# One engine instruction over two PSUM banks: four double tiles in place of eight single banks

## The chip, the cores and the metric

The kernel runs on one core of a Trainium2 chip. The metric is the device time of one execution in microseconds; lower is better. Engines are named as in the profile: PE (TensorE, matmuls), PEld (its weight loads), DVE (VectorE), ACT (ScalarE), POOL (GpSimd), SP (SyncE).

## What is computed

Sigmoid attention, then a gated feed-forward network over all tokens:

```python
batch, n_heads, seq, head_dim = (8, 12, 448, 64)
scale = 1.0 / np.sqrt(q.shape[-1])
scores = scale * np.matmul(q, k.transpose(0, 1, 3, 2)) - np.log(S)
attn = 1.0 / (1.0 + np.exp(-scores))
attn_out = np.matmul(attn, v)
x = attn_out.transpose(0, 2, 1, 3).reshape(B * S, H * D)      # 3584 x 768
gate = np.maximum(x @ w_gate, 0.0)                            # w_gate, w_val: 768 x 1536
val = x @ w_val
out = gate * val @ w_out                                      # w_out: 1536 x 768
```

Inputs and output are fp32; the kernel works in fp16 with fp32 accumulation in PSUM.

## The kernel before

The order on every engine is the program's own (`manual_schedule`); the framework adds the semaphores. A tile that takes over a buffer waits for the last accesses to the tile that held it before.

**PSUM.** There are eight banks of 512 fp32 per partition. During batch 0 four of them form a ring of single banks, `ring0`, and the other four are two double tiles of the pool `pairp`, for sigmoids over two banks (`FirstSlot.unit`, L270). At L634 `pairp` is closed and four further single banks, `ring1`, are opened in its place. From then on `bank(name)` hands out eight single banks in turn, and `later(order)` puts banks that stay in use for long at the end of the queue.

**Attention, batches 1 to 7.** The 12 heads are three groups of four. A *unit* (`qk_unit`, L292) makes the scores of one group against one seventh of the keys: four matmuls of 64x64 weights and 448 columns, which run beside each other in the array, into two banks; then ACT takes the sigmoid of each bank (L187). After seven units, `pv` (L242) multiplies by v with 28 such matmuls into two banks, and DVE copies each to `xT` (L184), scaled. The very last copy of batch 7 runs on ACT.

**Feed-forward.** Batches 0 and 1 (and 2) use `gv` (L304): six matmuls into a bank for the gate, six into another for the value, ReLU on ACT (L318) into `gate_sb`, and the product on DVE (L327) into `hT`. Later groups of two batches use `gv_pair` (L498): seven products of 2x2 blocks in place of eight, for two column blocks at once, in three pairs of banks `u`, `g2`, `g1` (in the code `b`, `c`, `a`), of which `b` is written four times. ACT or DVE copy (L524), DVE adds (L528), and DVE multiplies the gate by the value (L533), two instructions each, one for each bank. The sums of weights and tokens that this scheme needs (L376, L409, L479) are DVE's too. The output product is `down` (L341, banks `ya` and `yb`) or the seven-product `down_pair` (L423, banks `u`, `y12`, `y11`).

**The mix.** From batch 3 on, four or five units (with a `pv` after the second in every second stretch) are followed by one piece of feed-forward work, so that ACT works off its sigmoids while PE does large products. A `gv_pair` is 42 matmuls of 448 columns, a `down_pair` 42 of 384. In batches 1 and 2 the pieces are `gv`s (`ffn_mix`), and the sums of `w_out` (`weight_sums`) are queued on DVE between them as the weights come in. `gate_sums` runs on DVE once, in batch 3. `hold` makes POOL wait for a transposing DMA before it issues the next loads.

The queue of banks after a `gv_pair` is: two free banks, then `a`, `c`, `b`. After a `down_pair` it is: five free banks, then `a`, `c`, `b`.

Of the kernel before, what the change touches and what calls it, by code (L numbers as in the profile page):

```python
# [10 lines left out]
FP32 = mybir.dt.float32  # L11
# [6 lines left out]
def kernel(  # L18
# [36 lines left out]
    xTp = ctx.enter_context(tc.tile_pool(name="xTp", bufs=3))  # L55
    hTp = ctx.enter_context(tc.tile_pool(name="hTp", bufs=1))
    ysbp = ctx.enter_context(tc.tile_pool(name="ysbp", bufs=4))
    gsbp = ctx.enter_context(tc.tile_pool(name="gsbp", bufs=6))
    first_sbuf = ExitStack()
    early = first_sbuf.enter_context(tc.tile_pool(name="early", bufs=1))  # L60
    first_psum = ExitStack()
    free = deque()

    def open_banks(name):
        pool = ctx.enter_context(tc.tile_pool(name=name, bufs=1, space=bass.MemoryType.PSUM))
        free.extendleft((pool, f"{name}_{i}") for i in range(3, -1, -1))

    open_banks("ring0")
    pairp = first_psum.enter_context(
        tc.tile_pool(name="pairp", bufs=2, space=bass.MemoryType.PSUM)  # L70
    )
# [9 lines left out]
    def bank16(name):  # L81
        return bank(name, (P, 1024), FP16)

    def later(order):
        keys = [free[i - 8] for i in order]
        for key in keys:
            free.remove(key)
            free.append(key)

    in_tiles = {}
# [81 lines left out]
        for _ in range(count):  # L174
            nc.tensor.matmul(ps[:, 0:S], zeros[:, 0:P], zeros[:], start=True, stop=True)

    def put_xT(b, pr, q0, qn, src):
        if b not in xT_tiles:
            xT_tiles[b] = xTp.tile([P, NPAIR, S], FP16, tag="xT", name="xT")
        xT = xT_tiles[b][:, pr, q0 : q0 + qn]  # L180
        if b == B - 1 and pr == NPAIR - 1:
            nc.scalar.activation(xT, src, AF.Copy, scale=XSCALE)
        else:
            nc.vector.tensor_scalar(out=xT, in0=src, scalar1=XSCALE, scalar2=None, op0=AOP.mult)  # L184

    def sigmoid(PT_ap, ps_ap):
        nc.scalar.activation(PT_ap, ps_ap, AF.Sigmoid, bias=sig_bias, scale=qk_scale)  # L187


    def qkT_of(b, g):  # L190
        if (b, g) not in qkT_tiles:
            qkT_tiles[(b, g)] = qkTp.tile([P, TW, P], FP16, tag="qkT", name="qkT")
        return qkT_tiles[(b, g)]

    def pe_transposes(b, g, ti, c0=0, c1=NCH):
        t16 = in_tiles[b][ti]
        qkT = qkT_of(b, g)
        trt = bank16("trt")
        for c in range(c0, c1):
            for h in range(2):  # L200
                nc.tensor.transpose(
                    trt[64 * h : 64 * h + 64, c * P : (c + 1) * P],
                    t16[:, 2 * g + h, c * D : (c + 1) * D],
                    ident[:],
                )
# [35 lines left out]

    def pv(b, g, q0, qn, pieces):  # L242
        v16 = in_tiles[b][2]
        ps = [bank("pv_ps") for _ in range(2)]
        for c in range(NCH):
            for hh in range(2):
                for r in range(2):
                    o = row_of(r, hh)
                    rows = slice(o, o + 64)
                    nc.tensor.matmul(  # L250
                        ps[hh][64 * r : 64 * r + 64, 0:qn],
                        v16[rows, 2 * g + hh, c * D : (c + 1) * D],
                        pieces[c][rows, hh, :],
                        start=(c == 0),
                        stop=(c == NCH - 1),
                        tile_position=(o, 64 * r),
                        skip_group_check=True,
                    )
        for hh in range(2):
            put_xT(b, 2 * g + hh, q0, qn, ps[hh][:, 0:qn])  # L260


    class FirstSlot:
# [26 lines left out]
    PT_tiles = {}  # L290

    def qk_unit(b, g, c):  # L292
        ps = [bank("qk_ps") for _ in range(2)]
        qk(qkT_tiles[(b, g)], c, 0, NCH, lambda hh: ps[hh][:, 0:S])
        PT = PTp.tile([P, 2, S], FP16, tag="PT", name="PT")
        for hh in range(2):
            sigmoid(PT[:, hh, 0:S], ps[hh][:, 0:S])
        PT_tiles[(b, g, c)] = PT

    def pv_group(b, g):  # L300
# [1 line left out]


    def gv(b, q0, qn, f, act_relu):  # L304
        ps = []
        for nm, wt in (("g_ps", wg), ("v_ps", wv)):
            ps.append(bank(nm))
            for dc in range(NDC):
                nc.tensor.matmul(  # L309
                    ps[-1][:, 0:qn],  # L310
                    wt[:, dc, f * P : (f + 1) * P],
                    xT_tiles[b][:, dc, q0 : q0 + qn],
                    start=(dc == 0),
                    stop=(dc == NDC - 1),
                )
        gate_sb = gsbp.tile([P, S], FP32, tag="gsb", name="gate_sb")
# [10 lines left out]
        nc.vector.tensor_tensor(  # L327
            out=hT_tiles[g][:, f, o : o + qn],
            in0=gate_sb[:, 0:qn],
            in1=ps[1][:, 0:qn],  # L330
            op=AOP.mult,
        )
# [7 lines left out]

    def down(g, t):  # L341
        ysb = ysbp.tile([P, DM], FP32, tag="ysb", name="ysb")
        for nm, m0, m1 in (("ya", 0, 512), ("yb", 512, DM)):
            ps = bank(nm)
            for f in range(NFC):
                nc.tensor.matmul(  # L346
                    ps[:, 0 : m1 - m0],
                    hT_tiles[g][:, f, t * P : (t + 1) * P],
                    wo[:, f, m0:m1],
                    start=(f == 0),  # L350
                    stop=(f == NFC - 1),
                )
# [70 lines left out]
    def down_pair(g, p, beside, then, last, first_copy):  # L423
# [3 lines left out]
        B11, B21, B22 = wo[:, 0:HF, 0:HM], wo[:, HF:NFC, 0:HM], wo[:, HF:NFC, HM:DM]  # L427
        y1, y2 = (ysbp.tile([P, DM], FP32, tag="ysb", name="ysb") for _ in range(2))
        lo, hi = slice(0, HM), slice(HM, DM)
        b, c, a = bank("u"), bank("y12"), bank("y11")  # L430
        later((7, 6, 5))

        def product(ps, A, W, first=True):
            products([(ps, HM, HF, A, W, first)])
# [63 lines left out]
    def gv_pair(g, f, beside, first_copy):  # L498
        x1, x2 = xT_tiles[2 * g], xT_tiles[2 * g + 1]
        T1, T2, T4 = (late["X"][:, i] for i in range(3))  # L500
        B11, B21, T3, B22 = x1[:, 0:HD], x1[:, HD:NDC], x2[:, 0:HD], x2[:, HD:NDC]
        b, c, a = ([bank(nm) for _ in range(2)] for nm in ("u", "g2", "g1"))
        later((6, 7, 4, 5, 2, 3))
        gs = [[gsbp.tile([P, S], FP32, tag="gsb", name="gsb") for _ in range(3)] for _ in range(2)]
        if g not in hT_tiles:
            hT_tiles[g] = hTp.tile([P, NFC, 2 * S], FP16, tag="hT", name="hT")
        h = hT_tiles[g]
        sets = []
        for u in range(2):
            us, fs = slice(u * P, (u + 1) * P), slice((f + u) * P, (f + u + 1) * P)  # L510
            S1, S2, S4 = (t[:, :, us] for t in sums[("w", g, f)])
            sets.append((
                wg[:, 0:HD, fs], wg[:, HD:NDC, fs], wv[:, HD:NDC, fs],
                S1, S2, wv[:, 0:HD, fs], S4,
            ))
        del sums[("w", g, f)]

        def product(ps, i, W, first=True):
            for u in range(2):
                products([(ps[u], S, HD, sets[u][i], W, first)])  # L520

        def copy(i, ps, by=nc.scalar.copy):
            for u in range(2):
                by(gs[u][i][:], ps[u][:, 0:S])  # L524

        def plus(i, ps):
            for u in range(2):
                nc.vector.tensor_tensor(  # L528
                    out=gs[u][i][:], in0=ps[u][:, 0:S], in1=gs[u][i][:], op=AOP.add
                )  # L530

        def gated(u, o, gate_sb, val):
            nc.vector.scalar_tensor_tensor(  # L533
                out=h[:, f + u, o : o + S], in0=gate_sb, scalar=0.0, in1=val, op0=AOP.max, op1=AOP.mult
            )

        product(b, 0, B11)
        copy(0, b, first_copy)
        product(c, 3, T1)
        copy(2, c)  # L540
        product(b, 4, T2, False)
        copy(1, b)
        beside()
        product(a, 1, B21)
        plus(0, a)
        product(b, 5, T3, False)
        plus(2, b)
        product(c, 6, B22, False)
        plus(1, c)
        product(b, 2, T4, False)  # L550
        for u in range(2):
            gated(u, 0, gs[u][0][:], b[u][:, 0:S])
        for u in range(2):
            gated(u, S, gs[u][1][:], gs[u][2][:])

    gv_queue = deque()

# [73 lines left out]
        if b < 2:  # L631
            push_gv(b, 0, S, range(NFC))

    first_psum.close()  # L634
    open_banks("ring1")

    def hold(b, g):
        nc.gpsimd.tensor_copy(gate[0:1, :], qkT_tiles[(b, g)][0:1, 0, 0:2])
# [156 lines left out]
```

## Time and profile before

| | |
|---|---|
| median of 3 runs | 401.06 us (400.89 to 401.36) |
| span of the profiled execution, first to last instruction | 399.2 us |
| PE busy | 388.9 us (97%) |
| DVE busy | 279.9 us (70%) |
| ACT busy | 223.0 us (56%) |
| mean granted TensorE clock | 0.999 |

The profile gives the profiled execution's span alone; its own time is not listed, and what lies around the span is taken from the median: 401.06 - 399.2 = 1.86 us.

In the profile a line of a group names the line of the kernel, the engine, the operation, the tiles written and read, their shape, the count, and after the bar the busy time in us, the mean ns of one, and the idle time before them with what ended it. A line of the timeline gives the start in us from the beginning of the span, the length in us of the merged stretch, and the instruction with its count. A line of waits gives who waited for whom: us in total, times, and the longest. A busy PE is not PE at its peak, since the ends of matmuls are modelled; starts are recorded.

### The profile page before, as it was taken

How to read it: one execution, taken by the hardware profiler on the slowest of the kernel's cores; microseconds unless marked ns; L12 is line 12 of the kernel's file. 1: busy time of each engine (PE TensorE's matmuls, PEld its weight loads, DVE VectorE, ACT ScalarE, POOL GpSimd, SP SyncE). 2: the span in 40 equal slices, each digit the busy share in tenths (PEclk: the TensorE clock that was granted, in tenths of full speed). 3: DMA queues.
4: the chain of work that ended last, by engine and by line, in shares of the span. 5: the costliest groups of instructions: out<-in, count | busy, mean ns of one | idle time of the engine just before them, and what ended most of it. 6: DMA issues, size and time to landing. Idle time of an engine off the chain costs nothing.

```text
span 399.2 us, 8737 instructions
## 1 busy us (share of the span) xinstructions
PE 388.9 (97%) x3488; PEld 217.9 (55%) x3488; DVE 279.9 (70%) x539; ACT 223.0 (56%) x475; POOL 49.4 (12%) x73
## 2 busy tenths in 40 slices
PE   8999999999998999999999999999999999999994
PEld 3678786545455554554555555455455555555562
DVE  2454344367358889999758889999766779887661
ACT  5946778783885565655665455565566234533131
POOL 8643301600030300003000300000000000000000
PEclk9999999999999999999999999999999999999999
DMA  9999994999897894224945695223012320000144
GB/s 149 199 199 204 205 141 94 177 203 187 178 161 152 165 204 76 46 48 51 178 85 133 130 218 89 48 24 61 12 40 80 80 79 2 0 2 0 39 115 124
DMA packets 68793, 43.69 MB, mean 109 GB/s; under 512 B 35856, under 2 KB 65296, under 8 KB 68752
## 3 DMA queue, kind: packets, MB, share of 16 engines
q0 software_dynamic: 30736, 23.33, 39.1%
q1 hardware_dynamic: 37584, 19.24, 23.0%
q8 instruction: 27, 0.44, 0.5%
q10 hardware_dynamic: 432, 0.56, 0.4%
q14 instruction: 14, 0.11, 0.1%
HBM read 47.19 MB, written 11.01 MB: 146 GB/s over the span
## 4 chain that ended last, share of the span: by engine, by line
PE 73%; DMA 14%; issue 6%; POOL 3%; DVE 2%; ACT 1%; ACTq 0%; POOLq 0%; DVEq 0%
PE u L385 32%; PE g L385 15%; PE y L385 9%; DMA v<-in_v_dram 6%; PE qk_ps L232 5%; PE pv_ps L250 5%; DMA wo<-in_moe_w_out_dram 4%; DMA k<-in_k_dram 4%; PE ya L346 3%; PE v_ps L309 1%; PE yb L346 1%; PE g_ps L309 1%; POOL q L110 1%; POOL k L110 1%; DVE wv L376 1%
## 5 line engine op out<-in xcount | busy, mean ns | idle before, releaser
L187 ACT ACTIVATE PT<-qk_ps 128x448 f16<-128x448 f32 (+3 forms) x318 | 150.6, 594 | 71.2 <-PE qk_ps L232 71.1
L385 PEld LDWEIGHTS <-S 128*128 128x128 f16 x540 | 52.8, 98 | 44.4 <-issue 0.8
L528 DVE TENSOR_TENSOR gsb<-g,gsb 128x448 f32<-128x448 f32 x72 | 43.0, 625 | 14.5 <-PE g L385 13.8
L232 PE MATMUL qk_ps<-qkT 64*64 64x448 f16 (+2 forms) x756 | 50.0, 336 | 0.9 <-DVE qkT L206 0.5
L421 ACT ACTIVATE ysb<-u 128x384 f32<-128x384 f32 x27 | 13.4, 498 | 56.3 <-PE u L385 56.3
L327 DVE TENSOR_TENSOR hT<-gate_sb,v_ps 128x256 f16<-128x256 f32 (+2 forms) x36 | 16.2, 465 | 33.5 <-ACT gate_sb L318 22.4
L385 PEld LDWEIGHTS <-hT 128*128 128x128 f16 x288 | 27.7, 98 | 21.0 <-issue 3.2
L524 ACT COPY gsb<-u 128x448 f32<-128x448 f32 x48 | 25.8, 566 | 23.9 <-PE u L385 22.9
L250 PE MATMUL pv_ps<-PT,v 64*64 64x448 f16 (+2 forms) x756 | 37.4, 329 | 0.4 <-issue 0.4
L184 DVE TENSOR_SCALAR xT<-pv_ps 128x448 f16<-128x448 f32 (+2 forms) x53 | 27.9, 567 | 13.4 <-PE pv_ps L250 12.1
L232 PEld LDWEIGHTS <-qkT 64*64 64x64 f16 x756 | 20.3, 105 | 24.9 <-issue 16.3
L309 PE MATMUL v_ps<-xT,wv 128*128 128x256 f16 (+2 forms) x216 | 33.3, 291 | 0.4 <-DVE hT L327 0.2
L309 PE MATMUL g_ps<-xT,wg 128*128 128x256 f16 (+2 forms) x216 | 33.5, 292 | 0.1
L385 PEld LDWEIGHTS <-wv 128*128 128x128 f16 x216 | 21.1, 98 | 19.8
L385 PEld LDWEIGHTS <-wg 128*128 128x128 f16 x216 | 20.3, 98 | 20.6 <-issue 3.0
L250 PEld LDWEIGHTS <-v 64*64 64x64 f16 x756 | 21.8, 107 | 11.8 <-issue 1.4
L385 PE MATMUL u<-T,hT 128*128 128x384 f16 x144 | 27.3, 326 | 0.0
L437 DVE SCALAR_TENSOR_TENSOR ysb<-y,ysb 128x384 f32<-128x384 f32 x24 | 13.4, 557 | 18.8 <-PE y L385 11.3
L110 POOL DMA_DIRECT2D k<-in_k_dram x14 | 10.9, 779 | 112.3 <-DVE rel L215 105.8
L309 PEld LDWEIGHTS <-wg 128*128 128x128 f16 x216 | 18.5, 98 | 11.5 <-issue 5.0
L309 PEld LDWEIGHTS <-wv 128*128 128x128 f16 x216 | 20.1, 98 | 8.2 <-DMA wv<-in_moe_w_val_dram 0.5
L385 PE MATMUL u<-xT,wg 128*128 128x448 f16 x108 | 23.5, 353 | 0.1
(67 smaller groups left out, 531.3 us busy)
## 6 DMA issues: line engine op xcount, KB each, us to landing
out_dram<-ysb SPq DMA_DIRECT2D x53, 192.0 KB, 2.9
k<-in_k_dram POOLq DMA_DIRECT2D x5, 672.0 KB, 11.8
q<-in_q_dram POOLq DMA_DIRECT2D x5, 672.0 KB, 14.9
v<-in_v_dram POOLq DMA_DIRECT2D x8, 336.0 KB, 15.6
v<-in_v_dram POOLq DMA_DIRECT2D x16, 168.0 KB, 15.3
k<-in_k_dram POOLq DMA_DIRECT2D x8, 224.0 KB, 10.4
wo<-in_moe_w_out_dram POOLq DMA_DIRECT2D x1, 1536.0 KB, 13.2
q<-in_q_dram POOLq DMA_DIRECT2D x6, 224.0 KB, 11.3
```

Source lines behind the costliest of these rows:

```text
L110: nc.gpsimd.dma_start(t16[:, xs, cs], rows_of(src, b)[:, xs, cs])
L184: nc.vector.tensor_scalar(out=xT, in0=src, scalar1=XSCALE, scalar2=None, op0=AOP.mult)
L187: nc.scalar.activation(PT_ap, ps_ap, AF.Sigmoid, bias=sig_bias, scale=qk_scale)
L232: nc.tensor.matmul(out_of(hh)[o : o + 64, :], qkT[rows, c, cols], qkT[rows, NCH + c0 : NCH + c1, cols], start=True, stop=True, tile_positi ...
L250: nc.tensor.matmul(ps[hh][64 * r : 64 * r + 64, 0:qn], v16[rows, 2 * g + hh, c * D : (c + 1) * D], pieces[c][rows, hh, :], start=(c == 0), ...
L309: nc.tensor.matmul(ps[-1][:, 0:qn], wt[:, dc, f * P : (f + 1) * P], xT_tiles[b][:, dc, q0 : q0 + qn], start=(dc == 0), stop=(dc == NDC - 1),)
L327: nc.vector.tensor_tensor(out=hT_tiles[g][:, f, o : o + qn], in0=gate_sb[:, 0:qn], in1=ps[1][:, 0:qn], op=AOP.mult,)
L346: nc.tensor.matmul(ps[:, 0 : m1 - m0], hT_tiles[g][:, f, t * P : (t + 1) * P], wo[:, f, m0:m1], start=(f == 0), stop=(f == NFC - 1),)
L385: nc.tensor.matmul(ps[:, 0:n], A[:, k_, :], W[:, k_, :], start=(first and k_ == 0), stop=(k_ == kn - 1), skip_group_check=True,)
L421: nc.scalar.activation(o, ps[:, 0:HM], AF.Copy, scale=OUT_SCALE)
L524: by(gs[u][i][:], ps[u][:, 0:S])
L528: nc.vector.tensor_tensor(out=gs[u][i][:], in0=ps[u][:, 0:S], in1=gs[u][i][:], op=AOP.add)
```

## The change

From batch 1 on, all eight banks are one pool of four tiles of two banks, `doubles`. Both old pools, `ring0` and `pairp`, are closed before it opens. Every place that took two single banks takes a double tile, and one instruction works on both halves in these places: the sigmoid of a unit, the PV copy to `xT` (except the last), and in `gv_pair` the copy of `c`, the sums over `a` and over `c`, and the second product into `hT`. The copies of `b`, the sum over `b` and the product out of `b` stay two instructions. `down` has its two banks in one tile, and so do the transposes of k and q; in `down_pair`, `u` and `y12` share a tile and `y11` has one of its own with one half unused. `gsb` is three tiles of two halves in place of six tiles. The queue after a `gv_pair` is one free tile, then `a`, `c`, `b`; after a `down_pair` two free tiles, then `y11`, then `u` with `y12`.

```diff
-    gsbp = ctx.enter_context(tc.tile_pool(name="gsbp", bufs=6))
+    gsbp = ctx.enter_context(tc.tile_pool(name="gsbp", bufs=3))
...
-    open_banks("ring0")
+    ring0 = first_psum.enter_context(
+        tc.tile_pool(name="ring0", bufs=1, space=bass.MemoryType.PSUM)
+    )
+    free.extend((ring0, f"ring0_{i}") for i in range(4))
...
+    def open_doubles():
+        first_psum.close()
+        free.clear()
+        pool = ctx.enter_context(tc.tile_pool(name="doubles", bufs=1, space=bass.MemoryType.PSUM))
+        doubles.extend((pool, f"double{i}") for i in (2, 3, 0, 1))
+
+    def double(name, shape=(P, 2, 512), dtype=FP32):
+        pool, tag = doubles[0]
+        doubles.rotate(-1)
+        return pool.tile(list(shape), dtype, tag=tag, name=name)
...
+    def two_banks(name):
+        if doubles:
+            t = double(name)
+            return [t[:, 0, :], t[:, 1, :]], t
+        return [bank(name)[:] for _ in range(2)], None
...
-        trt = bank16("trt")
+        if doubles:
+            if ti == 0:
+                both_trt.append(double("trt", (P, 2, 1024), FP16))
+            trt = both_trt[-1][:, ti, :]
+        else:
+            trt = bank16("trt")
...
-        ps = [bank("pv_ps") for _ in range(2)]
+        ps, both_ps = two_banks("pv_ps")
...
-        for hh in range(2):
-            put_xT(b, 2 * g + hh, q0, qn, ps[hh][:, 0:qn])
+        last = b == B - 1 and g == NG - 1
+        if both_ps is None or last:
+            for hh in range(2):
+                put_xT(b, 2 * g + hh, q0, qn, ps[hh][:, 0:qn], last and hh == 1)
+        else:
+            put_xT(b, slice(2 * g, 2 * g + 2), q0, qn, both_ps[:, :, 0:qn])
...
-        ps = [bank("qk_ps") for _ in range(2)]
-        qk(qkT_tiles[(b, g)], c, 0, NCH, lambda hh: ps[hh][:, 0:S])
+        ps = double("qk_ps")
+        qk(qkT_tiles[(b, g)], c, 0, NCH, lambda hh: ps[:, hh, 0:S])
         PT = PTp.tile([P, 2, S], FP16, tag="PT", name="PT")
-        for hh in range(2):
-            sigmoid(PT[:, hh, 0:S], ps[hh][:, 0:S])
+        sigmoid(PT[:], ps[:, :, 0:S])
...
-        ps = []
-        for nm, wt in (("g_ps", wg), ("v_ps", wv)):
-            ps.append(bank(nm))
+        ps, _ = two_banks("gv_ps")
+        for i, wt in enumerate((wg, wv)):
...
-        for nm, m0, m1 in (("ya", 0, 512), ("yb", 512, DM)):
-            ps = bank(nm)
+        both_ps = double("y")
+        for i, (m0, m1) in enumerate(((0, 512), (512, DM))):
+            ps = both_ps[:, i, :]
...
-        b, c, a = bank("u"), bank("y12"), bank("y11")
-        later((7, 6, 5))
+        bc, aa = double("u"), double("y11")
+        later((3, 2))
+        b, c, a = bc[:, 0, :], bc[:, 1, :], aa[:, 0, :]
...
-        b, c, a = ([bank(nm) for _ in range(2)] for nm in ("u", "g2", "g1"))
-        later((6, 7, 4, 5, 2, 3))
-        gs = [[gsbp.tile([P, S], FP32, tag="gsb", name="gsb") for _ in range(3)] for _ in range(2)]
+        b, c, a = (double(nm) for nm in ("u", "g2", "g1"))
+        later((3, 2, 1))
+        gs = [gsbp.tile([P, 2, S], FP32, tag="gsb", name="gsb") for _ in range(3)]
...
+        whole = slice(0, 2)
         product(b, 0, B11)
-        copy(0, b, first_copy)
+        each(copy, 0, b, first_copy)
         product(c, 3, T1)
-        copy(2, c)
+        copy(whole, 2, c, nc.scalar.copy)
         product(b, 4, T2, False)
-        copy(1, b)
+        each(copy, 1, b, nc.scalar.copy)
         beside()
         product(a, 1, B21)
-        plus(0, a)
+        plus(whole, 0, a)
         product(b, 5, T3, False)
-        plus(2, b)
+        each(plus, 2, b)
         product(c, 6, B22, False)
-        plus(1, c)
+        plus(whole, 1, c)
         product(b, 2, T4, False)
-        for u in range(2):
-            gated(u, 0, gs[u][0][:], b[u][:, 0:S])
-        for u in range(2):
-            gated(u, S, gs[u][1][:], gs[u][2][:])
+        each(gated, 0, gs[0], b)
+        gated(whole, S, gs[1], gs[2])
...
-    first_psum.close()
-    open_banks("ring1")
+    open_doubles()
```

More of the change, by code (lines that the diff above doesn't have):

```diff
@@ L62 @@
     free = deque()
-    def open_banks(name):
-        pool = ctx.enter_context(tc.tile_pool(name=name, bufs=1, space=bass.MemoryType.PSUM))
-        free.extendleft((pool, f"{name}_{i}") for i in range(3, -1, -1))
-    open_banks("ring0")
+    ring0 = first_psum.enter_context(
+        tc.tile_pool(name="ring0", bufs=1, space=bass.MemoryType.PSUM)
+    )
+    free.extend((ring0, f"ring0_{i}") for i in range(4))
     pairp = first_psum.enter_context(
@@ L82, in bank16 @@
         return bank(name, (P, 1024), FP16)
+    doubles = deque()
+    def open_doubles():
[7 more added lines that the diff above has]
+        return pool.tile(list(shape), dtype, tag=tag, name=name)
     def later(order):
-        keys = [free[i - 8] for i in order]
+        keys = [doubles[i - 4] for i in order]
         for key in keys:
-            free.remove(key)
-            free.append(key)
+            doubles.remove(key)
+            doubles.append(key)
+    def two_banks(name):
[3 more added lines that the diff above has]
+        return [bank(name)[:] for _ in range(2)], None
     in_tiles = {}
@@ L175, in keep_warm, with put_xT @@
             nc.tensor.matmul(ps[:, 0:S], zeros[:, 0:P], zeros[:], start=True, stop=True)
-    def put_xT(b, pr, q0, qn, src):
+    def put_xT(b, prs, q0, qn, src, on_act=False):
         if b not in xT_tiles:
             xT_tiles[b] = xTp.tile([P, NPAIR, S], FP16, tag="xT", name="xT")
-        xT = xT_tiles[b][:, pr, q0 : q0 + qn]
-        if b == B - 1 and pr == NPAIR - 1:
+        xT = xT_tiles[b][:, prs, q0 : q0 + qn]
+        if on_act:
             nc.scalar.activation(xT, src, AF.Copy, scale=XSCALE)
@@ L193, in qkT_of @@
         return qkT_tiles[(b, g)]
+    both_trt = []
     def pe_transposes(b, g, ti, c0=0, c1=NCH):
@@ L304, in gv @@
     def gv(b, q0, qn, f, act_relu):
-        ps = []
-        for nm, wt in (("g_ps", wg), ("v_ps", wv)):
-            ps.append(bank(nm))
+        ps, _ = two_banks("gv_ps")
+        for i, wt in enumerate((wg, wv)):
             for dc in range(NDC):
                 nc.tensor.matmul(
-                    ps[-1][:, 0:qn],
+                    ps[i][:, 0:qn],
                     wt[:, dc, f * P : (f + 1) * P],
@@ L315, in gv @@
                 )
-        gate_sb = gsbp.tile([P, S], FP32, tag="gsb", name="gate_sb")
+        gate_sb = gsbp.tile([P, 2, S], FP32, tag="gsb", name="gate_sb")[:, 0, :]
         if act_relu:
@@ L519, in product, with each, copy, plus @@
             for u in range(2):
-                products([(ps[u], S, HD, sets[u][i], W, first)])
-        def copy(i, ps, by=nc.scalar.copy):
+                products([(ps[:, u, :], S, HD, sets[u][i], W, first)])
+        def each(job, *args):
             for u in range(2):
-                by(gs[u][i][:], ps[u][:, 0:S])
-        def plus(i, ps):
-            for u in range(2):
[L528 to L532, printed above, removed]
+                job(slice(u, u + 1), *args)
+        def copy(us, i, ps, by):
+            by(gs[i][:, us, :], ps[:, us, 0:S])
+        def plus(us, i, ps):
+            nc.vector.tensor_tensor(
+                out=gs[i][:, us, :], in0=ps[:, us, 0:S], in1=gs[i][:, us, :], op=AOP.add
+            )
+        def gated(us, o, gate_sb, val):
             nc.vector.scalar_tensor_tensor(
-                out=h[:, f + u, o : o + S], in0=gate_sb, scalar=0.0, in1=val, op0=AOP.max, op1=AOP.mult
+                out=h[:, f + us.start : f + us.stop, o : o + S],
+                in0=gate_sb[:, us, :], scalar=0.0, in1=val[:, us, 0:S],
+                op0=AOP.max, op1=AOP.mult,
             )
+        whole = slice(0, 2)
         product(b, 0, B11)
-        copy(0, b, first_copy)
+        each(copy, 0, b, first_copy)
         product(c, 3, T1)
-        copy(2, c)
+        copy(whole, 2, c, nc.scalar.copy)
         product(b, 4, T2, False)
-        copy(1, b)
+        each(copy, 1, b, nc.scalar.copy)
         beside()
         product(a, 1, B21)
-        plus(0, a)
+        plus(whole, 0, a)
         product(b, 5, T3, False)
-        plus(2, b)
+        each(plus, 2, b)
         product(c, 6, B22, False)
-        plus(1, c)
+        plus(whole, 1, c)
         product(b, 2, T4, False)
-        for u in range(2):
-            gated(u, 0, gs[u][0][:], b[u][:, 0:S])
-        for u in range(2):
-            gated(u, S, gs[u][1][:], gs[u][2][:])
+        each(gated, 0, gs[0], b)
+        gated(whole, S, gs[1], gs[2])
     gv_queue = deque()
```

## The prediction

> **What bounds the kernel now.** I read the engine totals first, then the waits, the groups by shape for prices, and last the timeline around the places where TensorE turns from attention to FFN products.
>
> ```profile
> PE 388.9 (97%) x3488; PEld 217.9 (55%) x3488; DVE 279.9 (70%) x539; ACT 223.0 (56%) x475; POOL 49.4 (12%) x73
> ```
>
> TensorE is busy for 97% of the span; ACT and DVE are not full. Work taken off those two is worth something only where TensorE waits for it.
>
> ```profile
> ACT PT L187 <- PE qk_ps L232: 71.1, 35, 4.4
> ```
>
> The longest wait of the sigmoids is for TensorE. In the waits TensorE itself hardly appears, because a lag under 150 ns counts as the pipeline's own; its short stalls must be read from starts. Columns below: start, length (us), instruction, count.
>
> ```profile
> 186.35 1.30 PE L385 MATMUL g<-xT,S 128*128 128x448 f16 x6
> 187.19 1.19 DVE L528 TENSOR_TENSOR gsb<-g,gsb 128x448 f32<-128x448 f32 x2
> 188.30 1.14 DVE L533 SCALAR_TENSOR_TENSOR hT<-gsb,u 128x448 f16<-128x448 f32 x2
> 188.72 1.16 PE L232 MATMUL qk_ps<-qkT 64*64 64x448 f16 x16
> 189.20 3.60 ACT L187 ACTIVATE PT<-qk_ps 128x448 f16<-128x448 f32 x8 [4.39 <-PE qk_ps L232]
> 189.81 1.31 PE L385 MATMUL u<-xT,wg 128*128 128x448 f16 x6
> ...
> 204.07 0.96 PE L232 MATMUL qk_ps<-qkT 64*64 64x448 f16 x16
> ...
> 204.56 0.98 ACT L187 ACTIVATE PT<-qk_ps 128x448 f16<-128x448 f32 x2 [2.61 <-PE qk_ps L232]
> ...
> 205.15 0.32 PE L385 MATMUL u<-wo,hT 128*128 128x384 f16 x1
> ```
>
> Four qk units fill eight banks, so `u` needs the bank of the first unit back. The first sigmoid runs 204.56 to 205.10 (one takes 0.54 here), `u` starts at 205.15: 0.05 after the release of one bank, while the second sigmoid runs until 205.54. Where nothing waits, `u` follows the last unit's start by 0.28 us (150.04 for two units, 0.19 apart, to 150.52). So the present order of banks lives on the early release of the first half, and the change takes that away.
>
> **Prices of the joined instructions.**
>
> ```profile
> L187 ACT ACTIVATE PT<-qk_ps 128x448 f16<-128x448 f32 x294 | 132.6, 575 | 63.0 <-PE qk_ps L232 63.0
> L187 ACT ACTIVATE PT<-qk_ps 128x1024 f16<-128x1024 f32 x9 | 8.6, 1025 | 2.3 <-PE qk_ps L232 2.3
> L187 ACT ACTIVATE PT<-qk_ps 128x768 f16<-128x768 f32 x9 | 6.9, 809 | 6.0 <-PE qk_ps L232 5.9
> L184 DVE TENSOR_SCALAR xT<-pv_ps 128x448 f16<-128x448 f32 x41 | 23.7, 619 | 9.8 <-PE pv_ps L250 8.6
> L184 DVE TENSOR_SCALAR xT<-pv_ps 128x256 f16<-128x256 f32 x6 | 2.3, 420 | 1.6 <-PE pv_ps L250 1.5
> ```
>
> A sigmoid of 896 lies midway between 768 and 1024: 0.92 us. Batch 0 runs such two-bank sigmoids already. The PV copy: (619-420)/192 = 1.04 ns an element, so 619 + 464 = 1.08 us; a sum goes from 0.63 to 1.09, a product from 0.62 to 1.08. 294 sigmoids become 147, each pair's 0.87 of ACT (two pitches of 0.43) becomes about 0.81: some 9 us off ACT; 74 DVE instructions fewer save about 0.1 each, 7 us. Both engines have idle time, so I put the direct gain at nothing. The cost is in the release: the first bank comes 0.92-0.54 = 0.38 us later from a sigmoid and 0.46 later from a PV copy; both banks together come only 0.06 to 0.08 earlier.
>
> In the Trainium skill, "Perfetto Trace Analysis", section "Optimizing Scalar/DVE Operations", grouping helps if the engine is saturated, with some 51 ns saved per ScalarE access to PSUM; 147 of them would be an estimated 7.5 us and 393.6. The same section advises breaking instructions up where unsaturated engines cause bubbles elsewhere, which speaks against this change; the rows (56%, and `u` 0.05 behind a release) meet this second condition, not the first.
>
> **The sum, block by block** (delay of the product after the block; the ring's order is unchanged, four tiles for eight banks).
>
> 1. Four units after a down pair or `down` (139.19, 204.07, 230.84, 295.71): `u` waits for the first sigmoid, 0.38 each: 1.52.
> 2. Four units after a gv pair (158.57, 188.72, 250.21, 280.36). The joined sum over `c` cannot start at 187.19 with its first bank but at 187.76, when its second is ready (186.35 + 1.30 + 0.11). It holds DVE 0.57 + 0.46 = 1.03, so the products out of `b` start at 188.79 and 189.32, the second ends at 189.94 (now 189.44). Unit 4 takes `b`'s tile at 189.98, `u` follows at 190.26 instead of 189.81: 0.45 each, 1.80. The sigmoid wait (190.17) hides inside.
> 3. Two units, PV, three units: `u` takes PV's tile. After a gv pair (167.71, 259.36) the same DVE chain lets the joined copy start at 169.83, not 169.64; it ends at 170.91 and `u` starts at 170.96, not 170.41: 0.55 each, 1.10. After a down pair (212.07, 303.71): copy from 214.00 to 215.08, `u` at 215.13 for 214.77: 0.36 each, 0.72. At 119.22 six weight sums hold DVE and the copy comes at 122.47: 0.46.
> 4. Two units, PV, two units (eight from 130.06 on): `u` takes the second unit's tile. At 148.31 its sigmoid would run 149.61 to 150.53, `u` natural at 150.52: 0.05 each, 0.40 (bounds 0 and 0.1).
> 5. Batches 1 and 2: the same first-sigmoid wait at 54.28 (0.37) and 114.05 (0.29); 105.71 costs 0.29 and gives 0.19 back at 109.25, where PV now waits for ACT's eighth sigmoid. 0.76.
> 6. The wait on `w_out`:
>
> ```profile
> 88.14 1.36 DVE L376 TENSOR_TENSOR T<-wo 128x2304 f16<-128x2304 f16 x1 [1.75 <-DMA wo<-in_moe_w_out_dram]
> 88.58 1.31 PE L309 MATMUL g_ps<-xT,wg 128*128 128x448 f16 x6
> 89.42 0.61 DVE L327 TENSOR_TENSOR hT<-gate_sb,v_ps 128x448 f16<-128x448 f32 x1
> 90.08 1.30 PE L309 MATMUL v_ps<-xT,wv 128*128 128x448 f16 x6 [0.20 <-DVE hT L327]
> ```
>
> This gv reuses the two banks of the gv three qk units before. Its `g` bank is freed early by ACT's ReLU; only `v` waits for the product that DVE holds back behind the weight sum. With one tile for both, `g` waits too: it starts at 90.08, `v` 1.14 later: 1.14 (bounds 0, if waits go by bank, and 1.5). DVE's next sums shift with it.
> 7. The change of pools.
>
> ```profile
> 32.08 0.58 PE L201 MATMUL trt<-ident,k 128*64 128x128 f16 x14
> 32.19 0.62 DVE L184 TENSOR_SCALAR xT<-pv_ps 128x192 f16<-128x192 f32 x2 [0.28 <-PE pv_ps L250]
> ```
>
> Now the transposes start in the pair tiles' banks while the old ring lives on. With the old ring closed too, a wait for the whole pool holds them until the PV copies end at 32.81: 0.78 (0 if it goes by address). A wait for `v`'s DMA at 47.4 (0.32) swallows part: 0.46.
>
> No charge: inside a gv pair the joined sum over `a` lets the sums over `b` end at about 187.05 and 187.6, and TensorE returns to these banks at 187.49 and 188.06; without that cover some 0.4 a pair. The six pairs at the end have the same slack and no units behind them. Three double `gsb` tiles hold what six did. `u` and `y12`, and the transposes of k and q, share a tile but not a bank, so I charge no wait. No DMA moves; the relayout copies and POOL's gate behind them shift with DVE.
>
> Sum: 1.52+1.80+1.10+0.72+0.46+0.40+0.76+1.14+0.46 = 8.36 us. The span of the profile is 399.2; the median of the runs, 401.06, lies 1.86 above, kept as it is: 399.2 + 8.36 + 1.86 = 409.4.
>
> **Rivals.** *Faster*: TensorE in truth waits for both banks, so a joined release comes earlier: some 16 stalled blocks times 0.07 = 1.1 us, 400.0. It decides if `u` now follows the second release; 205.15 against 205.54 speaks against it. Chance 0.08. *Absorbed*: the delays of items 1 to 3 land on spare time that the trace doesn't show, and none of 6 and 7 comes: 401.1, 0.04. *Half*: waits go by bank and address, so 6, 7 and 4 fall away (2.0): 407.4, chance 0.25. *Waits by whole tile inside a tile*: each product into `c` of a down pair would wait for the read of `b`, some three times 0.75 in 12 pairs: 27 us more, about 436; 0.04, because the change would then have to pay for every pair. *Forecast as summed*: 0.59.
>
> **How the numbers follow.** About 0.2% (0.8 us) can be told from no change. Slower by more: 0.59 + 0.25 + 0.04 = 0.88. Of the faster rival's 0.08 and the absorbed 0.04 I give 0.08 to faster and 0.04 to same. The range: below, the half case with 0.1 us less in each of the 13 waits of items 1 to 3 (406.1) and some of them overlapping, 404.5; above, items 4, 6, 7 at their upper bounds (+0.4, +0.36, +0.32) and 1 us for the pairs' cover, 411.5. It leaves out the faster, absorbed and whole-tile cases, 0.16.
>
> **What would show it.** Sigmoids of 128x896 near 0.92 us, ACT and DVE busy time down by some 9 and 7 us, yet a longer span; at the four-unit blocks `u` 0.05 after the end of the first joined sigmoid, or 0.28 behind a unit that waited for L533's pair; in the five-unit blocks `u` just after the joined xT copy; `g` waiting for DVE hT near 90 us; transposes late near 32.9. A span under 400, or blocks whose turn stays at 0.28, would prove me wrong; stalls inside down pairs would prove the whole-tile case.

## The result, and the profile after

The changed kernel takes 473.22 us (median of 6 runs, 472.82 to 478.45) against 401.09 us (6 runs, 400.78 to 401.75) in the same session: ratio 1.182, 95% interval 1.179 to 1.185. The forecast was 409.4 with a range to 411.5, so the sign was right and 64 us of the 72 were missed. The longest of the six runs had a mean granted clock of 0.982, the others 0.993 to 1.000. The profiled execution has a span of 471.1 us for 399.2 before.

The engine totals of the profile after, engine by engine busy time, share of the span and number of instructions:

```profile
PE 404.5 (86%) x3488; PEld 217.2 (46%) x3488; DVE 274.8 (58%) x465; ACT 213.8 (45%) x310; POOL 49.5 (11%) x73
```

The instructions went as the diff says, 165 fewer on ACT and 74 fewer on DVE, and both engines are less busy, by 9.2 and 5.1 us. TensorE runs the same 3488 matmuls and its share fell from 97% to 86%: it waits. (Its busy time grew because matmul ends are modelled: a product of six is drawn 1.14 us long where the next one can start after 0.97, and each wait lays bare the difference.) The chain that ended last, by engine, says on whom:

```profile
PE 65%; DVE 22%; ACT 7%; issue 3%; DMA 1%; DVEq 0%; ACTq 0%
```

Before, DVE held 2% of that chain and ACT 1%. Two of the groups that the forecast priced by interpolation, kept apart by shape, came out at 919 ns (forecast 0.92 us) and 1088 ns (1.09):

```profile
L204 ACT ACTIVATE PT<-qk_ps 128x896 f16<-128x896 f32 x147 | 124.3, 919 | 63.5 <-PE qk_ps L256 63.5
...
L558 DVE TENSOR_TENSOR gsb<-g,gsb 128x896 f32<-128x896 f32 x36 | 39.2, 1088 | 21.4 <-PE g L412 21.4
```

What is new is in the waits. In the list of before, no row of TensorE's matmuls was above 1.2 us; after, these rows are there (who waits for whom: us in total, times, longest; L412 writes all products by the seven-product schemes, L373 `down`, L225 the transposes, L335 `gv`):

```profile
PE u L412 <- DVE ysb L465: 17.1, 24, 0.7
PE u L412 <- ACT ysb L448: 8.8, 15, 0.6
PE u L412 <- DVE ysb L443: 7.2, 9, 2.0
PE y L373 <- DVE ysb L380: 5.0, 4, 2.1
PE u L412 <- DVE xT L201: 4.1, 5, 1.7
PE u L412 <- DVE gsb L558: 3.2, 18, 0.2
PE trt L225 <- DVE qkT L230: 2.6, 3, 0.9
...
PE gv_ps L335 <- DVE hT L353: 2.2, 5, 0.6
```

The first three are inside the down pairs: 24 = 12 pairs times 2 for the sums at L465, and the 15 and 9 for the copies at L448 and L443 make another 24. (These rows count idle time from the modelled end of the product before, so they come to less than the lateness of the starts, which is used below.) The fourth is inside `down`, the sixth inside the gv pairs, the seventh between the transposes of k and of q. One down pair in the timeline (start, length, instruction, idle time before it and who ended it; `u` and `y12` are both named `u` now, the name of their tile):

```profile
137.51 0.56 DVE L443 TENSOR_SCALAR ysb<-u 128x384 f32<-128x384 f32 x1 [1.23 <-PE u L412]
...
138.12 1.14 PE L412 MATMUL u<-T,S 128*128 128x384 f16 x6 [0.65 <-DVE ysb L443]
...
139.29 0.49 ACT L448 ACTIVATE ysb<-u 128x384 f32<-128x384 f32 x1 [2.62 <-PE u L412]
139.84 1.14 PE L412 MATMUL u<-T,S 128*128 128x384 f16 x6 [0.58 <-ACT ysb L448]
...
140.81 1.14 PE L412 MATMUL y<-wo,hT 128*128 128x384 f16 x6
...
141.78 1.14 PE L412 MATMUL u<-T,hT 128*128 128x384 f16 x6
...
143.02 0.56 DVE L465 SCALAR_TENSOR_TENSOR ysb<-u,ysb 128x384 f32<-128x384 f32 x1 [0.47 <-PE u L412]
143.62 1.14 PE L412 MATMUL u<-wo,S 128*128 128x384 f16 x6 [0.70 <-DVE ysb L465]
...
144.87 0.56 DVE L465 SCALAR_TENSOR_TENSOR ysb<-u,ysb 128x384 f32<-128x384 f32 x1 [1.29 <-PE u L412]
...
145.48 1.14 PE L412 MATMUL u<-T,hT 128*128 128x384 f16 x6 [0.72 <-DVE ysb L465]
```

Without a wait the products follow each other every 0.97 us (139.84, 140.81, 141.78). The product into `y12` at 138.12 starts 0.05 after the copy out of `b`, another bank, has ended (138.07); the next product into `b` at 139.84 starts 0.06 after the copy out of `y12`. It happens four times in a pair, and each time the start comes 0.75 to 0.9 late against the 0.97. Only the product `y` at 140.81 and the one after it run free: `y11` has a tile of its own, and gives the copy out of `b` the time it needs.

The blocks in which the forecast had looked for its loss did behave as written. The four-unit block that stood at 204.07 before:

```profile
231.68 0.97 PE L256 MATMUL qk_ps<-qkT 64*64 64x448 f16 x16
...
232.12 1.73 ACT L204 ACTIVATE PT<-qk_ps 128x896 f16<-128x896 f32 x2 [4.01 <-PE qk_ps L256]
...
233.08 0.81 PE L412 MATMUL u<-wo,hT 128*128 128x384 f16 x4 [0.43 <-ACT PT L204]
```

The first of the two joined sigmoids takes 0.92 and ends at 233.03, and `u` starts 0.05 later: the same lag as before, behind a later release. And the change of pools, where the copies of PV hold the transposes until 32.48 + 0.62 = 33.10:

```profile
32.48 0.62 DVE L201 TENSOR_SCALAR xT<-pv_ps 128x192 f16<-128x192 f32 x2 [0.28 <-PE pv_ps L274]
...
33.15 0.58 PE L225 MATMUL trt<-ident,k 128*64 128x128 f16 x14 [0.71 <-DVE xT L201]
```

**Where the 72 us lie.** I took the distance from each matmul's start to the next and subtracted the time that its columns take where nothing waits (for six matmuls of 384 columns the 0.97 us above). This excess is 24.8 us in all before and 97.4 after. The increase of 72.6 divides into: between products of down pairs 40.0; inside gv pairs 12.5; between the halves of `down` 6.0; transposes of q behind the copy of k 3.2; after blocks of attention units 10.4, the forecast's place; change of pools 0.75. That is 72.9; small decreases elsewhere make the difference. One of them is 0.31 at the wait for a DMA near 47.4 that item 7 of the forecast had named; the others I did not follow.

### The profile page after: what moved, and what is told of

It is laid out like the page before. It is cut to its first block, busy times and chain, and to the rows that moved or that the text cites. A ratio compares the mean times of both kernels' runs of the same rounds, so it can differ in the third digit from the quotient of the medians.

```text
span 471.1 us, 8305 instructions
## 1 busy us (share of the span) xinstructions
PE 404.5 (86%) x3488; PEld 217.2 (46%) x3488; DVE 274.8 (58%) x465; ACT 213.8 (45%) x310; POOL 49.5 (11%) x73
## 4 chain that ended last, share of the span: by engine, by line
PE 65%; DVE 22%; ACT 7%; issue 3%; DMA 1%; DVEq 0%; ACTq 0%
PE u L412 35%; PE gv_ps L335 12%; PE g L412 5%; PE pv_ps L274 5%; DVE gsb L558 4%; DVE hT L563 4%; PE qk_ps L256 4%; ACT PT L204 3%; DVE gsb L555 3%; DVE ysb L465 3%; PE y L412 2%; ACT ysb L448 2%; PE y L373 2%; DVE xT L201 2%; ACT gate_sb L344 2%
## 5 line engine op out<-in xcount | busy, mean ns | idle before, releaser
L204 ACT ACTIVATE PT<-qk_ps 128x896 f16<-128x896 f32 (+4 forms) x171 | 142.3, 906 | 71.9 <-PE qk_ps L256 71.9
L412 PEld LDWEIGHTS <-S 128*128 128x128 f16 x540 | 52.5, 97 | 78.6 <-issue 38.8
L448 ACT ACTIVATE ysb<-u 128x384 f32<-128x384 f32 x39 | 19.2, 491 | 106.7 <-PE u L412 103.1
L558 DVE TENSOR_TENSOR gsb<-g,gsb 128x896 f32<-128x896 f32 x36 | 39.2, 1088 | 21.4 <-PE g L412 21.4
L412 PEld LDWEIGHTS <-hT 128*128 128x128 f16 x288 | 27.9, 97 | 33.6 <-issue 16.8
L412 PE MATMUL u<-T,S 128*128 128x384 f16 x144 | 27.2, 325 | 16.1 <-ACT ysb L448 8.8
L353 DVE TENSOR_TENSOR hT<-gate_sb,gv_ps 128x256 f16<-128x256 f32 (+2 forms) x36 | 16.5, 465 | 40.9 <-ACT gate_sb L344 39.5
L201 DVE TENSOR_SCALAR xT<-pv_ps 128x896 f16<-128x896 f32 (+3 forms) x33 | 26.5, 819 | 17.0 <-PE pv_ps L274 17.0
L335 PE MATMUL gv_ps<-xT,wg 128*128 128x256 f16 (+2 forms) x216 | 33.5, 290 | 2.6 <-DVE hT L353 2.2
L412 PE MATMUL u<-T,hT 128*128 128x384 f16 x144 | 27.3, 325 | 8.6 <-DVE ysb L465 8.6
L412 PEld LDWEIGHTS <-wv 128*128 128x128 f16 x216 | 20.9, 97 | 28.0 <-issue 11.4
L335 PE MATMUL gv_ps<-xT,wv 128*128 128x256 f16 (+2 forms) x216 | 33.3, 290 | 0.0
L412 PEld LDWEIGHTS <-wg 128*128 128x128 f16 x216 | 20.5, 98 | 22.7 <-issue 5.2
L465 DVE SCALAR_TENSOR_TENSOR ysb<-y,ysb 128x384 f32<-128x384 f32 x12 | 6.7, 558 | 34.1 <-PE y L412 24.6
L412 PE MATMUL u<-X,wv 128*128 128x448 f16 x108 | 23.3, 351 | 3.2 <-DVE gsb L558 3.2
L335 PEld LDWEIGHTS <-wg 128*128 128x128 f16 x216 | 19.2, 97 | 14.1 <-issue 7.2
L465 DVE SCALAR_TENSOR_TENSOR ysb<-u,ysb 128x384 f32<-128x384 f32 x24 | 13.4, 558 | 20.7 <-PE u L412 20.7
## 6 DMA issues: line engine op xcount, KB each, us to landing
k<-in_k_dram POOLq DMA_DIRECT2D x8, 224.0 KB, 10.4
```

Source lines behind the costliest of these rows:

```text
L335: nc.tensor.matmul(ps[i][:, 0:qn], wt[:, dc, f * P : (f + 1) * P], xT_tiles[b][:, dc, q0 : q0 + qn], start=(dc == 0), stop=(dc == NDC - 1),)
L353: nc.vector.tensor_tensor(out=hT_tiles[g][:, f, o : o + qn], in0=gate_sb[:, 0:qn], in1=ps[1][:, 0:qn], op=AOP.mult,)
L412: nc.tensor.matmul(ps[:, 0:n], A[:, k_, :], W[:, k_, :], start=(first and k_ == 0), stop=(k_ == kn - 1), skip_group_check=True,)
L448: nc.scalar.activation(o, ps[:, 0:HM], AF.Copy, scale=OUT_SCALE)
L465: nc.vector.scalar_tensor_tensor(out=o, in0=ps[:, 0:HM], scalar=OUT_SCALE, in1=o, op0=AOP.mult, op1=AOP.add)
L558: nc.vector.tensor_tensor(out=gs[i][:, us, :], in0=ps[:, us, 0:S], in1=gs[i][:, us, :], op=AOP.add)
```

## The experiments

Theory A: the semaphores go by the whole PSUM tile, so an instruction on one half waits for all that was done to the other half, reads and writes alike, and each place where a tile's halves are worked by turns pays for it. Rival B: the joined instructions, which release later, are the cost. A predicts that the loss stays when all joined instructions are split again, B that it goes. Then the places of theory A are undone one after the other.

**The joined instructions split again, tiles kept.**

```diff
-        sigmoid(PT[:], ps[:, :, 0:S])
+        for hh in range(2):
+            sigmoid(PT[:, hh, 0:S], ps[:, hh, 0:S])
...
-        copy(whole, 2, c, nc.scalar.copy)
+        each(copy, 2, c, nc.scalar.copy)
```

and the same for the PV copy, the sums over `a` and `c` and the second product.

> Every sigmoid, PV copy, sum and product is again two instructions, the double tiles stay. Theory A: the tiles alone make the loss, so nothing is won: 473 us, 469 to 479. Theory B (the joined instructions make it): back to 401 to 406 us.

Measured: 478.59 us (476.74 to 478.91), ratio to before 1.192 (1.190 to 1.195). TensorE's waits stand as they were:

```profile
PE u L413 <- DVE ysb L466: 17.4, 24, 1.1
PE u L413 <- ACT ysb L449: 8.9, 15, 0.6
PE u L413 <- DVE ysb L444: 7.2, 9, 2.0
```

B falls. The tiles alone make the kernel 77 us slower, and joining the instructions gives some 3 us of it back. The medians differ by 5.4, but these four runs had a granted clock of 0.989 to 0.993: of the 5.9 us between the two profiled spans (477.0 and 471.1), 2.8 lie inside products, chiefly in two stretches of 3.4 us (near 104 and 439) at half the clock, and 3.1 at the turns from one product or block to the next.

**Down pairs: three tiles.**

```diff
-        bc, aa = double("u"), double("y11")
-        later((3, 2))
-        b, c, a = bc[:, 0, :], bc[:, 1, :], aa[:, 0, :]
+        b, c, a = (double(nm)[:, 0, :] for nm in ("u", "y12", "y11"))
+        later((3, 2, 1))
```

> Theory A (waits go by the whole tile, so a product into one bank of a double waits for the reader of the other): with y12 in a double of its own, the four stalls inside each of the 12 down pairs (0.81, 0.74, 0.87 and 0.88 us, 3.3 together, 41 us in all) go; 473.2 - 41 = 432 us, range 429 to 436, since three of four tiles are now held. Theory B (the loss is the late release of joined reads and the short ring of four tiles, as forecast but larger): the stalls stay and one more tile is held; 473 us or more.

Measured: 434.47 us (433.77 to 435.66), ratio 1.084 (1.081 to 1.086): 38.75 us less than after. Who TensorE waits for, in this kernel:

```profile
PE y L373 <- DVE ysb L380: 5.0, 4, 2.1
PE u L412 <- DVE xT L201: 4.1, 5, 1.7
PE u L412 <- DVE gsb L557: 3.2, 18, 0.2
...
PE u L412 <- DVE ysb L443: 1.1, 1, 1.1
```

The waits for the two sums and for ACT's copies are gone from the list (the last row is one wait in the first pair, 0.6 in the list of before), the excess inside down pairs is 2.3 us (1.2 before, 41.2 after), and the three other rows stand as they were. The products of a pair follow each other without a stall:

```profile
132.22 1.14 PE L412 MATMUL u<-wo,hT 128*128 128x384 f16 x6 [1.74 <-DVE xT L201]
133.19 1.14 PE L412 MATMUL y<-T,S 128*128 128x384 f16 x6
134.17 1.14 PE L412 MATMUL u<-T,S 128*128 128x384 f16 x6
```

More than half of the loss is one pair of banks in one tile. A ring of four tiles that is too short can't have been the cause: this kernel holds one tile more in each down pair.

**And `down` and the transposes with a tile for each bank.** The kernel above, with

```diff
-        both_ps = double("y")
-        for i, (m0, m1) in enumerate(((0, 512), (512, DM))):
-            ps = both_ps[:, i, :]
+        for m0, m1 in ((0, 512), (512, DM)):
+            ps = double("y")[:, 0, :]
...
-            if ti == 0:
-                both_trt.append(double("trt", (P, 2, 1024), FP16))
-            trt = both_trt[-1][:, ti, :]
+            trt = double("trt", (P, 2, 1024), FP16)[:, 0, :]
```

> As the first, and the two banks of down and the transposes of k and q get doubles of their own too. Theory A: the stalls of ya to yb (5 downs of 1.2 us, 6 us) and of the transposes (3 of 0.9 us, 2.6 us) go as well: 432 - 8.6 = 423 us, 420 to 428. Theory B: 473 us or more.

Measured: 424.6 us (424.32 to 424.84), ratio 1.059 (1.057 to 1.061), 9.87 us less, against 9.2 of excess that the trace had shown there; the rows of `y` behind L380 and of the transposes behind `qkT` are gone from the list. Unlike the down pair's, neither place works its halves by turns: the second half is written once, but the framework makes it wait for the copy out of the first (5.0 us in four waits, the longest, 2.1, where DVE has token sums ahead of that copy).

**And the pair of banks of a gv pair that is written four times.** The kernel above, with two tiles for `b`; `c` and `a` stay double and joined:

```diff
-        b, c, a = (double(nm) for nm in ("u", "g2", "g1"))
-        later((3, 2, 1))
+        b = [double("u")[:, 0, :] for _ in range(2)]
+        c, a = double("g2"), double("g1")
+        later((3, 2, 0, 1))
```

> As the third, and in each gv pair the two banks of b have doubles of their own (a and c stay joined). Theory A: the three stalls in each of 18 gv pairs (0.27, 0.12, 0.34 us; 13.3 us) go; PV then meets b's tile about 0.3 us early in 8 stretches (2.4) and the six pairs at the end, which hold all four tiles, wait some 0.5 us each for c (2.5): 423 - 13.3 + 4.9 = 415 us, 410 to 419. What is left above the kernel before, 8 to 18 us, is the late release that was forecast (8.4) and the gv's own waits. Theory B: 473 us or more.

Measured: 417.25 us (416.71 to 417.5), ratio 1.040 (1.039 to 1.042), 7.35 us less. The place looks like this in the kernel after, timeline:

```profile
321.13 1.30 PE L412 MATMUL g<-xT,S 128*128 128x448 f16 x6
321.40 1.16 DVE L558 TENSOR_TENSOR gsb<-u,gsb 128x448 f32<-128x448 f32 x2 [0.24 <-PE u L412]
...
322.61 1.30 PE L412 MATMUL u<-X,wv 128*128 128x448 f16 x6 [0.18 <-DVE gsb L558]
```

The last product into `b` waits until DVE has summed both halves (321.40 + 1.16 = 322.56), where one half would have been enough. With two tiles the 12.5 us of excess between `g` and `u` are 0, but four tiles then serve as a ring of which one gv pair holds all. Eight PV blocks behind a pair start 0.3 us later each (490 ns behind the last matmul of the units, 179 without this edit), 2.5 together, and ten of the twelve pairs between attention blocks wait at their own first products, 3.5 together; other waits of the blocks are 0.9 shorter. That makes 12.5 into about the 7.35 measured. The six pairs at the end, where the expectation had placed 2.5 us, have no stall.

**And the gate and the value of `gv` in two tiles.** The kernel above, with

```diff
-        ps, _ = two_banks("gv_ps")
         for i, wt in enumerate((wg, wv)):
+            ps.append(double("gv_ps")[:, 0, :] if doubles else bank("gv_ps")[:])
```

> The third of the series: as the kernel with own tiles for down pairs, down, transposes and the written-four-times pair of banks, and with the gate and the value of the single column blocks (batches 0 to 2) in double tiles of their own, half of each unused. Theory A (waits go by the whole tile, so the ReLU of the gate waits until the value's matmuls have run, and the gate's bank comes back late): the ReLU starts 1.3 us sooner, the stalls of 0.66 us ahead of the gate products shrink, total 414 (412 to 417) against 417.25. Rival B (the gate's ReLU was late for another reason, and the ring, which now holds two more tiles per column block, is only shorter): 417 to 421.

Measured: 418.79 us (418.15 to 419.01), ratio 1.044 (1.042 to 1.045): 1.5 us more, where A had expected 3 less; the time lies where rival B had it. Of A the mechanism holds. In the kernel after the ReLU on the gate's half begins when the value's matmuls are through (74.04 + 1.30 = 75.34):

```profile
74.04 1.30 PE L335 MATMUL gv_ps<-xT,wv 128*128 128x448 f16 x6
...
75.38 0.54 ACT L344 ACTIVATE gate_sb<-gv_ps 128x448 f32<-128x448 f32 x1 [1.73 <-PE gv_ps L335]
```

and here 0.20 after the value's first:

```profile
72.90 1.30 PE L334 MATMUL gv_ps<-xT,wv 128*128 128x448 f16 x6
...
73.10 0.54 ACT L343 ACTIVATE gate_sb<-gv_ps 128x448 f32<-128x448 f32 x1 [1.64 <-PE gv_ps L334]
```

So a read of one half waits for a write of the other too. But the time did not come: the `gv`s behind a block still lose 6.6 us (7.4 without this edit; 1.4 of it is now one wait for the product on DVE near 92), and 3.8 appear inside the `gv`s, where without it there were 0.2. TensorE's list has nine waits of `gv_ps` for a sigmoid, 1.7 us: with a tile more for each column block, the ring of four comes round to units whose sigmoids are still running.

**Tile by tile at the change of pools.** The kernel after, with the pool's `reuse_waits="tile"`.

> The kernel after, with the pool of double tiles told to wait tile by tile for what held its banks, not for everything in the two closed pools. Theory A (the change of pools holds the first transposes until the last copies out of the old ring have ended, as forecast in item 7): the transposes after batch 0 start about 0.75 us sooner after the last matmul of batch 0 than in the kernel after, nothing else moves but a later DMA wait that takes some of it back; total 0.4 to 0.8 us less than 473.2. Rival B (the 0.75 us there come from somewhere else, the copy of k before the transposes of q for instance): the transposes start where they do now, total 473.2.

One run, 476.32 us at a mean granted clock of 0.985 (0.997 in the profile after), so its total says nothing; the place does:

```profile
32.32 0.58 PE L225 MATMUL trt<-ident,k 128*64 128x128 f16 x14
32.43 0.62 DVE L201 TENSOR_SCALAR xT<-pv_ps 128x192 f16<-128x192 f32 x2 [0.28 <-PE pv_ps L274]
...
33.64 0.58 PE L225 MATMUL trt<-ident,q 128*64 128x128 f16 x14 [0.73 <-DVE qkT L230]
```

The transposes of k start 0.70 after PV's start at 31.62, where it was 33.15 - 31.67 = 1.48: the 0.78 of item 7, shown. The last line is the whole-tile wait of the transposes of q.

**Two edits of the kernel before.** Reading for the forecast had shown two waits that owe nothing to the banks: six weight sums on DVE ahead of the copies to `xT` at 122.47, and the sums of `w_out` at 88.

```diff
             if b == 3 and m == 3:
-                for f in range(0, NFC, 2):
-                    gate_sums(f, f + 2)
+                jobs.append(lambda: [gate_sums(f, f + 2) for f in range(0, NFC, 2)])
```

so that they are queued beside the last `down` and not behind it.

> Not the change, but a wait that the profile of before shows at 119.22: the kernel before, with the six sums of the weights of batch 3 put on VectorE ahead of the last output product of that stretch, not behind it, so that the copies to xT at 122.47 no longer stand behind them. Before's 1.5 us of stall ahead of u there should shrink to about 0.3: 399.9 us (399.3 to 400.4) against 401.1. If the sums only push something else back (the copies out of that output product, or the hT products), 401 or above.

Measured: 399.79 us (399.55 to 400.41) against 401.17 (400.39 to 401.97), ratio 0.9969 (0.9959 to 0.9979). The timeline of this kernel:

```profile
120.78 1.04 PE L232 MATMUL qk_ps<-qkT 64*64 64x448 f16 x12
120.99 1.16 DVE L184 TENSOR_SCALAR xT<-pv_ps 128x448 f16<-128x448 f32 x2 [0.44 <-PE pv_ps L250]
...
121.76 1.15 PE L385 MATMUL u<-wo,hT 128*128 128x384 f16 x6
```

`u` starts 0.98 after the last three units began; in the kernel before it was 123.14 - 120.94 = 2.20. The 1.22 account for nearly all of the 1.38 measured.

The second adds a new share-out of the sums of `w_out` and one copy on ACT:

```diff
-                4: [(1, lambda: weight_sums(0)), (0, lambda: weight_sums(1))],
-                5: [(1, lambda: weight_sums(2)), (0, lambda: weight_sums(3))],
+                4: [(0, lambda: weight_sums(0))],
+                5: [(2, lambda: weight_sums(1)), (1, lambda: weight_sums(2)), (0, lambda: weight_sums(3))],
...
-                next_work(jobs)
+                next_work(jobs, True)
```

> As the run before this one, and with the sums of w_out shared out differently between the column blocks of batch 2 (two of them earlier in the stretch whose waits they cause, at 88 us) and the first copy of the first down pair on ScalarE in place of VectorE, which is behind the sums. 399.2 us (398.6 to 400) if both waits shrink, 399.9 as the run before this one if neither does, above that if the sums that were moved now stand in front of the hT products of another column block.

Measured: 399.26 us (398.75 to 399.92), ratio 0.9952 (0.9938 to 0.9966): faster than both kernels of the case. The interval overlaps that of the run before it, so the second step's 0.5 us is likely, not shown.

## Why the prediction was wrong

**The step that failed** is the sentence "`u` and `y12`, and the transposes of k and q, share a tile but not a bank, so I charge no wait", with "inside a gv pair the joined sum over `a` lets the sums over `b` end" early enough beside it. Both counted waits by bank; `down`, whose halves share a tile as well, the forecast did not name. The runs show waits by tile: 38.75 us for `u` and `y12`, 9.87 for `down` and the transposes, and 12.5 us of excess inside gv pairs (7.35 net). Nothing in the trace of before stood behind the zero: it has no PSUM tile whose two banks are written and read by turns. Item 6 of the same sum did go by tile ("With one tile for both, `g` waits too"), for a tile that changes hands, and items 4, 6 and 7 have a bound on either side. This cost had none in the sum or its range; its far end was four stalls of 0.8 in each of 12 pairs.

**The rival that came true** was on the page: "Waits by whole tile inside a tile", 436 us, at 0.04. Its reason for the low chance, "because the change would then have to pay for every pair", is a consequence and no evidence. Its price was low for three reasons: it counted three stalls of 0.75 in a down pair, where there are four and they cost 0.83 on average (27 against 40.0 us); it left out gv pairs, `down` and the transposes, the same case in other places (21.7 us); and it left out reads that wait for writes of the other half. It did name the sign that tells it, stalls inside down pairs.

**By items**, the growth of the excess in the block and at the product behind it (blocks by their starts before):

| item | forecast, us | measured, us |
|---|---|---|
| 1, four units after a down pair or `down` | 4 x 0.38 | 0.38, 0.37, 0.32, 0.32 |
| 2, four units after a gv pair | 4 x 0.45 | 0.54, 0.54, 0.63, 0.63 |
| 3, PV and three units | 2 x 0.55, 2 x 0.36, 0.46 | 2 x 0.61, 2 x 0.39, 0.47 |
| 4, PV and two units | 8 x 0.05 | 4 x 0.06, 4 x 0 |
| 5, batches 1 and 2 (54.28; 105.71 with 109.25; 114.05) | 0.37; 0.10; 0.29 | 0.38; 0.53; 0.51 |
| 6, `gv` behind three units (70.16; 80.23; 87.88) | 0; 0; 1.14 | 0.66; 0.66; 0.66 |
| 7, change of pools | 0.78 | 0.78 |

So the late release was foreseen in size: the sum of 8.36 us stands against 10.4 + 0.75 in the trace, of which 0.71 is in three blocks of batch 1 (34.08, 37.85 and 42.95) that the forecast did not charge. But it was laid on the joined instructions, and that is not what the runs show. With every instruction split again and the tiles kept, the blocks of item 1 turn 0.43 to 0.44 later than before and those of item 3 by 0.75 and 0.46 (0.54 at 119.22): more than joined, not less. There too the cost is the tile, which makes `u` wait for both halves; the joined instruction shortens that wait. Item 2 came as near as it did by luck, through another chain than the forecast's. In the block that stood at 188.72 before, the joined sum over `c` ends at 213.46, 0.28 ahead of the block, and the products out of `b` don't wait for it. DVE sits idle until the matmuls into both halves of `b` are through, again a wait by tile:

```profile
213.74 0.76 PE L256 MATMUL qk_ps<-qkT 64*64 64x448 f16 x12
213.85 1.15 DVE L563 SCALAR_TENSOR_TENSOR hT<-gsb,u 128x448 f16<-128x448 f32 x2 [0.39 <-PE u L412]
```

Item 6 was right in its mechanism, the gate's half waiting for the product on DVE, and wrong in its place: it was charged at 88.58 alone, where weight sums delay that product, but the ReLU that now waits for the value delays it in other blocks too (the row `gv_ps` behind `hT`: five waits, 2.2 us).

**The faster rival** was right about one thing: where the waiting engine needs both halves, one instruction releases sooner than two. Split again, the kernel loses some 3 us more at its turns. Its condition, that before already waited so, was false: `u` there followed the first release. In the Trainium skill, "Perfetto Trace Analysis", section "Optimizing Scalar/DVE Operations", work on engines that are not saturated but cause bubbles elsewhere may gain from being broken up. Here breaking up made the bubbles longer, by those 3 us, since the wait goes by a tile of both banks. Whether it helps where each bank is waited for by itself no run here shows: no kernel joins the instructions over two tiles.

**What remains** at 417.25, 16.1 us above before, are the late releases by tile of items 1 to 5, 7 and `gv`, and about 5 us that half-empty tiles cost in a ring of four. No version with double tiles came under the kernel with eight banks.

## What to carry to other kernels

Before two buffers are put into one tile for the sake of one wide instruction, list every other instruction on either half, and ask what it waits for if a wait means the whole tile; the loss is largest where the halves were a double buffer (write one, read the other). An operation that the old trace cannot show gets both ends of its cost in the range, above all when it is repeated: 0.8 us is small, 48 times it is 40. A rival that explains itself with "that would be bad" needs a row of the profile for or against it, or a larger chance.

## What the runs showed that was not expected

- PSUM waits went by the tile in both directions: matmuls into one half waited for copies out of the other (0.05 to 0.06 behind their end), and a ReLU on one half began 0.04 behind matmuls into the other. These are the program's semaphores, not a limit of the banks: in the trace, the first matmul at 138.12 waits for the semaphore that DVE's copy counts up (number 100), and with three tiles in a down pair the same product, at 133.19, waits for ACT's instead (104) and starts before DVE's copy does.
- Joining two sigmoids of 448 columns saves ACT 0.06 us (132.6 us of busy time became 124.3 over 147 pairs) and puts the end of the first bank's work 0.38 later (919 ns against 0.54). The forecast took this second figure for the price, but in double tiles nothing waits for the first bank alone: split again, the four-unit blocks turn 0.44 later than before, joined 0.32 to 0.38.
- Within double tiles the joined instructions were worth some 3 us, though neither ACT (45%) nor DVE (58%) is near full: the wait there is for the release of both halves.
